# Attention values on column tiles of TensorE, with the result turned to tokens by the DMA crossbar

## The chip, the cores and the metric

The kernel runs on one core of one Trainium2 chip. The metric is the device time of one execution in microseconds, as the median over runs. The core has five engines that run their own instruction lists and meet at semaphores: TensorE (PE in the profile, with its weight loads as PEld), VectorE (DVE), ScalarE (ACT), GpSimd (POOL) and SyncE (SP), which here only issues DMAs.

## The reference

Two layers, each an attention block and a feed-forward block, over 2048 tokens of width 640. The attention has 32 heads of width 20 and cuts the tokens into 4 segments of 512. Inside a segment it is ordinary causal attention; what lies before a segment comes through a memory matrix per head:

```
x = x + A(layernorm(x)); x = x + B(layernorm(x))      # twice
A: q, k, v = x@wq, x@wk, x@wv        # 32 heads of 20
   for each segment s of 512 tokens:
     p     = softmax(q k^T / sqrt(20) + causal mask);  a_dot = p v
     a_mem = phi(q) M / (phi(q) z + 1e-6)              # phi(t) = t+1 for t>0, else exp(t)
     o     = g*a_mem + (1-g)*a_dot                     # g = sigmoid(beta) per head
     M += phi(k)^T v;  z += sum phi(k)
   return o @ wo
B: relu(x@w1) @ w2                   # 640 -> 1728 -> 640
```

All inputs and the output are bf16.

## The kernel before

Everything stays in SBUF between the stages; x is held as 16 tiles of 128 tokens (`x_sb`). The work goes by segment: normalise (`lnorm`, transposing the normed tokens to `xnT` by DMA), project to keys and queries with the features on partitions (`proj_kq`, line 712) and to values with the tokens on partitions (`proj_v`, line 746), score and apply, project the output (`out_proj`, line 1102), normalise again, and the feed-forward block (`ffn`, lines 1150 and 1170).

Heads are kept four to a group: keys and queries of head group g lie at partitions 0, 32, 64 and 96, 20 rows each. `scores` (line 978) takes two groups, a pair, in five rounds; a round is four or eight matmuls on four row tiles of the array, 512 columns in each tile, into PSUM banks 0 to 3. The scores come out with the keys on partitions. ScalarE takes the exponential (lines 994 and 998) into `PT`, of which there are two, one for each group of the pair, and GpSimd sets the part above the diagonal to zero (line 967). `PT` of one group holds four heads, and for each block j of 128 keys the queries from 128j on.

`apply` (line 1027) multiplies by the values. For a block i of 128 queries and a block j of 128 keys with j <= i, the 128x128 block of `PT` is the stationary operand, and the 20 values of the head with one more column (`v_aug`, whose last column gives the softmax sum, scaled so that the gate is in it) stream past: 40 matmuls with 21 columns for one group, into one PSUM bank (`OD`), with the tokens on partitions. VectorE takes the reciprocal of the sums (line 1042), multiplies (line 1050, or 1045 in a layer's first segment), and adds the product to the part that came from the memory (line 1055), in `o_sb`. When all eight groups of a segment are in, `o_turn` (line 1092) transposes `o_sb` to `oT` by DMA for `out_proj`.

The order of the instructions on each engine is fixed before the kernel runs, by a planner in the file (`Sched`, `paced`, `each`). Each stage is a stream of operations with a due time in units of a segment; the planner holds estimates of the duration of every operation, keeps a clock per engine, and always takes the operation that can start first, the one due first where several can start. A change of the array's tiling mode is booked at 100 ns (`MODE_NS`). Operations that would be in the way of a score round are put behind it (`RESERVE`). Scores and applies are due long before everything else; normalising and the projections of segment k are due 1.0 to 0.2 segments before it, the feed-forward block 1.4 to 2.4 segments after. Besides, a segment's normalising waits until the scores of the segment two before have begun, and until one of two `xnT` places is free. Buffers are slots that a stage takes and drops: two for `PT`, one for `OD`, three banks (`MISC`) for all other PSUM results, three sets of keys, queries and values, three normed tiles (`NXN`). SP issues all transposes, the relay of the last three key groups through DRAM (`relay`, lines 774 and 787) and the output, in the planned order, and waits at each for what it needs.

Of the kernel before, what the change touches and what calls it, by code (L numbers as in the profile page):

```python
# [11 lines left out]
H = 32  # L12
# [146 lines left out]


class Sched:
# [66 lines left out]
    def _best(self, op, resv=None):  # L228
# [140 lines left out]
def bass_interleave_layers__memory_aug_infini_attn__dense_activation_relu__prompt_kernel(  # L369
    nc, A_x, A_wq, A_wk, A_wv, A_wo, A_beta, B_x, B_w1, B_w2, out,  # L370
):
    with contextlib.ExitStack() as es:
# [6 lines left out]
        NXT, NXN, NET = 3, 3, 2  # L379
# [10 lines left out]
        NKQ, NVA = 2 * 5 * L, NJ * H * E1  # L390
        kq_0 = wb[:, W1N:W1N + NKQ].rearrange("p (n c f) -> p n c f", n=2, c=5)
        va_0 = wb[:, W1N + NKQ:W1N + NKQ + NVA].rearrange("p (j h e) -> p j h e", j=NJ, h=H)
# [18 lines left out]
        va_12 = sb("va_12", [128, 2, NJ, H, E1])  # L411
        v_aug = [va_0, va_12[:, 0], va_12[:, 1]]
# [7 lines left out]
        otmp = sb("otmp", [128, 2, NJ, 4, DH])  # L420
        rden = sb("rden", [128, 2, NJ, 4, 1], dt.float32)
# [22 lines left out]
        OTMP = [Slot(otmp[:, k], "otmp") for k in range(2)]  # L444
# [7 lines left out]
        ktk_sem = [sem_("kt%d" % k) for k in range(3)]  # L452
        ot_sem = [sem_("ot%d" % k) for k in range(2)]
# [98 lines left out]
        def consts():  # L552
# [4 lines left out]
            S.set("ident", v=[t1])  # L557
            th = yield pool(150, lambda e: e.memset(nhalf[:], -0.5))
# [8 lines left out]
            for b in range(3):  # L567
                t = yield pool(400, lambda e, b=b: e.tensor_copy(
                    v_aug[b][:, :, :, DH:E1], gt[:, 1, :][:, None, :, None].to_broadcast([128, NJ, H, 1])), [ta])
                VA[b][0].drop(t)  # L570
# [373 lines left out]
        def scores(m):  # L944
# [27 lines left out]
            for u, parts in enumerate(rounds):  # L972
# [10 lines left out]
                items = sorted({x for x, _, _ in parts})  # L983
                w = []
# [27 lines left out]
        def apply(n):  # L1012
# [10 lines left out]
            tk = od = None  # L1023
            for i in range(NJ):
                def make(bank, i=i, x=n % 2):
                    od = bank[:, 0:336].rearrange("p (i hh e) -> p i hh e", i=NJ, hh=4)
                    return [(lambda e, i=i, hh=hh, j=j: e.matmul(  # L1027
                        od[:, i, hh, :], PT[:, x, hh, PT_OFF[j] + 128 * (i - j):PT_OFF[j] + 128 * (i - j) + 128],
                        v_aug[b][:, j, 8 * hh + g, :], start=(j == 0), stop=(j == i)),
                        i == NJ - 1 and hh == 3 and j == i) for hh in range(4) for j in range(i + 1)]  # L1030
                if od is None:
# [225 lines left out]
```

## Time and profile before

| | |
|---|---|
| Median of 3 runs | 639.55 us (639.46 to 642.18) |
| Profiled execution | 639.16 us, span 637.4 us, mean granted clock 0.973 |
| PE | 593.1 us busy, 93% of the span |
| ACT | 424.7 us, 67% |
| DVE | 392.7 us, 62% |
| POOL | 197.8 us, 31% |
| DMA queue of SP | 32.5 MB, 29.6% of the 16 engines' span |

"Busy" is the time in which the engine had an instruction under way. Matmuls are pipelined: each is shown with its whole latency, while the next begins long before it ends, so 93% is not 93% of what PE could stream. In a row of a group stand the engine, the operation, what it writes and reads with the shapes, the number of instructions, the total busy time and the mean of one in ns, and behind the second bar the idle time of the engine just before them with what ended it. "xnT<-xn_tok" is a write of `xnT` that reads `xn_tok`.

### The profile page before, as it was taken

To read this page: it belongs to the slowest core of one execution; us is meant where nothing else is said; L and a number is where in the kernel's file an instruction comes from. 1 tells how busy PE (TensorE), PEld (TensorE's weight loads), DVE (VectorE), ACT (ScalarE), POOL (GpSimd) and SP (SyncE) were. 2 spreads that over 40 slices of the span, in tenths; PEclk is the share of its full clock that TensorE was granted. 3 is DMA by queue.
4 is the path that set the end of the run, shared out by engine and by line. 5 is a ranking of instruction groups with operands and counts; after the bars stand their busy time and mean duration, and the time that the engine had idled before them with its cause. 6 is when DMAs were issued, how large, how long until landed. Compare 5 with 4: busy or idle time off the path is not lost.

```text
span 637.4 us, 15205 instructions
## 1 busy us (share of the span) xinstructions
PE 593.1 (93%) x6498; PEld 337.8 (53%) x6498; DVE 392.7 (62%) x995; ACT 424.7 (67%) x512; POOL 197.8 (31%) x318
## 2 busy tenths in 40 slices
PE   6868998699999999999999999999999999999798
PEld 3344554354565566545664556645565556646445
DVE  7457768884588469646765567867586465735302
ACT  4576977787867766678677857878578756780040
POOL 3244344533334334333433313333233322330000
PEclk9878997899999999999999999999999999999799
DMA  6398749620322152222712426023530126004201
GB/s 196 92 173 155 116 102 174 126 51 16 72 48 59 15 91 33 48 38 37 121 24 43 75 32 98 11 43 75 87 84 11 22 25 113 33 1 63 63 0 42
DMA packets 101940, 43.17 MB, mean 68 GB/s; under 512 B 88416, under 2 KB 100576, under 8 KB 101872
## 3 DMA queue, kind: packets, MB, share of 16 engines
q1 hardware_dynamic: 98240, 32.52, 29.6%
q0 software_dynamic: 1520, 7.21, 4.0%
q10 hardware_dynamic: 2112, 2.47, 1.1%
q8 instruction: 51, 0.84, 0.5%
q14 instruction: 17, 0.14, 0.1%
HBM read 14.26 MB, written 6.55 MB: 33 GB/s over the span
## 4 chain that ended last, share of the span: by engine, by line
PE 73%; DVE 11%; ACT 7%; DMA 5%; POOL 2%; issue 1%; SPq 0%; DVEq 0%
PE ps L1150 18%; PE ps L1170 16%; PE ps L712 11%; PE ps L1027 9%; PE ps L978 7%; PE ps L1102 6%; PE ps L746 5%; ACT PT L998 4%; DMA oT<-o_sb 2%; DMA xnT<-xn_tok 2%; DVE x_sb L1065 1%; DVE xn_tok L627 1%; POOL rstd L623 1%; DVE stats L615 1%; POOL PT L967 1%
## 5 line engine op out<-in xcount | busy, mean ns | idle before, releaser
L998 ACT ACTIVATE PT<-ps 128x1024 bf16<-128x1024 f32 x256 | 248.1, 1022 | 90.2 <-PE ps L978 89.6
L967 POOL TENSOR_SCALAR_AFFINE_SELECT PT<-PT 128x512 bf16<-128x512 bf16 x256 | 162.0, 650 | 340.8 <-ACT PT L998 302.0
L1150 PE MATMUL ps<-xnT,wb 128*128 128x512 bf16 x560 | 150.6, 385 | 6.0 <-DMA xnT<-xn_tok 4.2
L1170 PE MATMUL ps<-wb,hT 128*128 128x320 bf16 x896 | 138.2, 299 | 3.7 <-DVE o_sb L914 2.5
L1170 PEld LDWEIGHTS ps<-wb,hT 128*128 128x128 bf16 x896 | 82.6, 98 | 43.0 <-issue 7.8
L1065 DVE TENSOR_TENSOR x_sb<-x_sb,ps 128x320 bf16<-128x320 bf16 x128 | 60.7, 479 | 62.1 <-PE ps L1170 50.5
L1150 PEld LDWEIGHTS ps<-xnT,wb 128*128 128x128 bf16 x560 | 51.7, 99 | 68.2 <-issue 16.5
L1134 ACT ACTIVATE hT<-ps 128x512 bf16<-128x512 f32 x69 | 41.3, 598 | 62.2 <-PE ps L1150 61.5
L746 PE MATMUL ps<-wv_r,xnT 128*128 128x320 bf16 x320 | 73.1, 306 | 3.5 <-ACT xnT L643 2.3
L1027 PEld LDWEIGHTS ps<-va,PT 128*128 128x128 bf16 x2240 | 64.1, 96 | 13.2 <-POOL PT L967 5.3
L994 ACT ACTIVATE PT<-ps 128x1024 bf16<-128x1024 f32 x64 | 62.0, 1022 | 12.1 <-PE ps L978 12.1
L1027 PE MATMUL ps<-va,PT 128*128 128x21 bf16 x2240 | 65.2, 173 | 2.6 <-POOL PT L967 2.5
L712 PE MATMUL ps<-xnT,wk_p 128*128 128x512 bf16 x200 | 63.8, 396 | 0.9 <-ACT xnT L643 0.8
L1042 DVE RECIPROCAL rden<-ps 128x16 f32<-128x16 f32 x64 | 16.2, 254 | 77.7 <-PE ps L1027 77.7
L712 PE MATMUL ps<-xnT,wq_p 128*128 128x512 bf16 x200 | 60.8, 387 | 0.9 <-DVE kq L699 0.9
L1102 PE MATMUL ps<-wo_r,oT 128*128 128x320 bf16 x320 | 54.1, 308 | 6.3 <-DMA oT<-o_sb 2.9
L699 DVE CAST kq<-ps 128x512 bf16<-128x512 f32 x54 | 36.8, 685 | 20.2 <-PE ps L712 20.0
L627 DVE TENSOR_SCALAR xn_tok<-x_sb,mv,rstd 128x640 bf16<-128x640 bf16 x64 | 33.0, 526 | 25.8 <-POOL rstd L623 17.3
L746 PEld LDWEIGHTS ps<-wv_r,xnT 128*128 128x128 bf16 x320 | 30.4, 99 | 28.2 <-issue 4.9
L1102 PEld LDWEIGHTS ps<-wo_r,oT 128*128 128x128 bf16 x320 | 29.3, 99 | 25.3 <-DMA oT<-o_sb 4.7
L1133 DVE TENSOR_SCALAR hT<-ps 128x512 bf16<-128x512 f32 x43 | 29.7, 690 | 19.7 <-PE ps L1150 19.4
L978 PE MATMUL ps<-kq 20*128 20x512 bf16 (+3 forms) x560 | 36.1, 308 | 2.8 <-ACT PT L998 2.6
(79 smaller groups left out, 548.2 us busy)
## 6 DMA issues: line engine op xcount, KB each, us to landing
kqL<-kq_scr SPq DMA_DIRECT2D x32, 120.0 KB
kq_scr<-kq SPq DMA_DIRECT2D x28, 120.0 KB
out_dram<-x_sb SPq DMA_DIRECT2D x16, 160.0 KB, 1.8
wb<-in_B_w_dram POOLq DMA_DIRECT2D x5, 432.0 KB, 6.7
x_sb<-in_A_x_dram POOLq DMA_DIRECT2D x3, 640.0 KB, 5.1
wb<-in_B_w_dram POOLq DMA_DIRECT2D x2, 640.0 KB, 6.6
xnT<-xn_tok SPq DMA_TRANSPOSE x60, 2.7
wv_r<-in_A_wv_dram ACTq DMA_DIRECT2D x1, 800.0 KB, 6.0
```

The lines of the kernel that those rows point to most:

```text
L712: fn = lambda e, bank, k=k, w_p=w_p, c=c: e.matmul(bank, w_p[:, k, c * 128:(c + 1) * 128], xnT[:, k_, :, k, :], start=(k == 0), stop=(k == ...
L746: fn = lambda e, bank, k=k, i=i, hf=hf: e.matmul(bank[:, 0:320], xnT[:, k_, i, k, :], wv_r[:, k, hf * 320:(hf + 1) * 320], start=(k == 0), ...
L967: tm = yield pool(590.0, lambda e: e.affine_select(out=reg, in_=reg, pattern=[[0, 4], [1, 128]], compare_op=ALU.is_ge, fill=0.0, base=0, c ...
L978: fns.append((lambda e, x=x, j=j, hh=hh, N=N, o=o: e.matmul(ps[:, hh, o:o + N], kq(b, gg[x], 0)[32 * hh:32 * hh + DH, 128 * j:128 * j + 12 ...
L994: fn = lambda e, k=k, bp=bs.ap: e.activation(PT[:, :, 2 * k:2 * k + 2, 1024:1280], bp.rearrange("p h (x t) -> p x h t", x=2), ACT.Exp, sca ...
L998: fn = lambda e, k=k, bp=bs.ap, x=items[0], c0=c0: e.activation(PT[:, x, 2 * k:2 * k + 2, c0:c0 + 512], bp, ACT.Exp, scale=SCALE)
L1027: return [(lambda e, i=i, hh=hh, j=j: e.matmul(od[:, i, hh, :], PT[:, x, hh, PT_OFF[j] + 128 * (i - j):PT_OFF[j] + 128 * (i - j) + 128], v ...
L1065: ta = yield dve(320, 1, lambda e: e.tensor_tensor(xa, xa, bk.ap[:, 0:320], ALU.add), [tk], early=HOT)
L1102: fn = lambda e, bank, k=k, hf=hf, o=ot.ap: e.matmul(bank[:, 0:320], o[:, k, :], wo_r[:, k, hf * 320:(hf + 1) * 320], start=(k == 0), stop ...
L1134: lambda e: e.activation(hTv[:, dc, :], bk.ap, ACT.Relu), [tk] + hs.old)
L1150: fn = lambda e, bank, k=k, dc=dc: e.matmul(bank, w1_r[:, k, dc * 128:(dc + 1) * 128], xnT[:, k_, :, k, :], start=(k == 0), stop=(k == FC ...
L1170: fn = lambda e, bank, dc=dc, i=i, hf=hf: e.matmul(bank[:, 0:320], hTv[:, dc, i * 128:(i + 1) * 128], w2_r[:, dc, hf * 320:(hf + 1) * 320] ...
```

## The change

The operands of the apply change places. For head hh of the group and key block j, the values are now the stationary operand: 32 columns from the head's first value on, that is its 20 values, its sum column and 11 columns that belong to the next head and come out unused. They sit in column tile hh of the array (128 rows, 32 columns), and write to PSUM partitions 32hh to 32hh+31. The streaming operand is `PT` of the block, with all queries from 128j on: 512, 384, 256 and 128 columns for j = 0 to 3. So an apply is 16 matmuls, four in each column tile, marked as mode "col". The result has head and feature on partitions and the tokens along the free dimension. So that the 32 columns of the last head don't run out of the buffer, each value buffer is 16 elements longer, zeroed by GpSimd at the start.

The result must be turned to tokens. `turn` evacuates the bank to bf16 (`oraw`, on VectorE or ScalarE, whichever the planner finds sooner), and when both groups of a pair are there, one DMA transpose of 128x1024 (`XK`) brings them to `otok` with the tokens on partitions. Then come one reciprocal for both groups, and in a layer's first segment two products into `o_sb`, else one product in place and two sums.

In the planner, a column operation that finds the array in the full mode is ranked 3 us later (`PATIENCE`), so that it tends to come behind a score round. A pair's score rounds take each of the two `PT` halves when they first write it, where before both were taken ahead of the first round. Normalising, projections and relay are due 1.5 segments earlier. One of the three normed tiles is gone.

```diff
+PATIENCE = 3000.0
@@ Sched._best
             if e == "pe" and op.mode != self.mode:
                 start = max(self.free[e] + MODE_NS, r)
+                if op.mode == "col" and self.mode == "full":
+                    rank = max(rank, r + PATIENCE)
@@ buffers
-        NXT, NXN, NET = 3, 3, 2
+        NXT, NXN, NET = 3, 2, 2
-        NKQ, NVA = 2 * 5 * L, NJ * H * E1
+        NKQ, NVA = 2 * 5 * L, NJ * H * E1 + 16
-        otmp = sb("otmp", [128, 2, NJ, 4, DH])
-        rden = sb("rden", [128, 2, NJ, 4, 1], dt.float32)
+        oraw = sb("oraw", [128, 2, 2, L])
+        otok = sb("otok", [128, 2, 2 * NJ, 4, 32])
+        rden = sb("rden", [128, 2, 2 * NJ, 4, 1], dt.float32)
@@ scores
-            for x in range(2):
-                yield Op([("act", 0.0, 0.0, lambda: [])], [], hold=[PTS[x][0]])
-            pold = [PTS[x][0].old for x in range(2)]
+            pold = [None, None]
...
                 items = sorted({x for x, _, _ in parts})
+                for x in items:
+                    if pold[x] is None:
+                        yield Op([("act", 0.0, 0.0, lambda: [])], [], hold=[PTS[x][0]])
+                        pold[x] = PTS[x][0].old
@@ apply
-            for i in range(NJ):
...
+            x = n % 2
+            def make(bank):
+                return [(lambda e, hh=hh, j=j: e.matmul(
+                    bank[32 * hh:32 * hh + 32, 128 * j:L],
+                    v_flat[b][:, (j * H + 8 * hh + g) * E1:(j * H + 8 * hh + g) * E1 + 32],
+                    PT[:, x, hh, PT_OFF[j]:PT_OFF[j] + L - 128 * j], start=(j == 0), stop=(j == NJ - 1)),
+                    j == NJ - 1 and hh == 3) for j in range(NJ) for hh in range(4)]
+            tk, od = yield pe(25.0 + 1280 / 2.4, make, mk + vt, [OD], mode="col")
...
+            S.spawn(turn(n, a, s, g, od, tk), "turn")
+        def turn(n, a, s, g, od, tk):
+            x = n % 2
+            if x == 0:
+                te, rw = yield evac(512, 1, lambda e, d: e.tensor_copy(d[:, 0, :], od.ap),
+                                    lambda e, d: e.activation(d[:, 0, :], od.ap, ACT.Copy), [tk], [ORAW])
+                od.drop(te)
+                S.set("raw", n, v=[rw, te])
+                return
+            rw, t0 = yield Need("raw", n - 1)
+            te = yield evac(512, 1, lambda e: e.tensor_copy(rw.ap[:, 1, :], od.ap),
+                            lambda e: e.activation(rw.ap[:, 1, :], od.ap, ACT.Copy), [tk] + rw.old)
+            od.drop(te)
+            tx, ok = yield XK(rw, [t0, te])
+            rw.drop(tx)
+            ov = otok[:, ok.ap]
+            tr, rd = yield dve(240, 1, lambda e, d: e.reciprocal(d, ov[:, :, :, DH:E1]), [tx], [RDEN])
+            ob = yield Need("ob", a, s)
+            num = ov[:, :, :, 0:DH]
...
+            if s == 0:
...
+            else:
+                tm = yield dve(640, 1, lambda e: e.tensor_tensor(
+                    num, num, rd.ap.to_broadcast([128, 2 * NJ, 4, DH]), ALU.mult), [tr])
+                om = yield Need("omem", a, s, g // 4)
...
+        class XK(Op):
+            def __init__(self, rw, waits):
+                super().__init__([("sp", 200.0 + 27.0 * 64, 0.0, self.make)], waits, [OTOK], 1)
+                self.dma = [None, 900.0, 1700.0]
...
+                return [(lambda e: e.dma_start_transpose(
+                    otok[:, k].rearrange("p c r e -> p c (r e)"), rw.ap.rearrange("p x t -> p (x t)")), True)]
@@ due times
-        each(ln1, "ln1", -1.0, -0.8, 24)
-        each(proj_kq, "kq", -0.8, -0.3, 60)
-        each(relay, "relay", -0.4, -0.3, 8)
-        each(proj_v, "v", -0.8, -0.2, 48)
+        each(ln1, "ln1", -2.5, -2.3, 24)
+        each(proj_kq, "kq", -2.3, -1.8, 60)
+        each(relay, "relay", -1.9, -1.8, 8)
+        each(proj_v, "v", -2.3, -1.7, 48)
```

More of the change, by code (lines that the diff above doesn't have):

```diff
@@ L443, in bass_interleave_layers__memory_aug_infini_attn__dense_activation_relu__prompt_kernel @@
         OSB = [[Slot(o_sb[:, k], "osb")] for k in range(2)]
-        OTMP = [Slot(otmp[:, k], "otmp") for k in range(2)]
+        ORAW = [Slot(oraw[:, k], "oraw") for k in range(2)]
+        OTOK = [Slot(k, "otok") for k in range(2)]
         RDEN = [Slot(rden[:, k], "rden") for k in range(2)]
@@ L557, in consts @@
             S.set("ident", v=[t1])
+            tv0 = []
+            for b in range(3):
+                tk = yield pool(100, lambda e, b=b: e.memset(v_flat[b][:, NJ * H * E1:NVA], 0.0))
+                tv0.append(tk)
             th = yield pool(150, lambda e: e.memset(nhalf[:], -0.5))
@@ L1022, in apply @@
             va, vt = vt[0], vt[1:]
-            tk = od = None
-            for i in range(NJ):
[L1025 to L1031, printed above, removed]
-                    _, od = yield pe(26.0 * 4, make, mk + vt, [OD])
-                else:
-                    tk = yield pe(26.0 * 4 * (i + 1), lambda make=make, bank=od.ap: make(bank))
+            x = n % 2
[6 more added lines that the diff above has]
+            tk, od = yield pe(25.0 + 1280 / 2.4, make, mk + vt, [OD], mode="col")
             pt.drop(tk)
```

51 lines of the change are left out of this document (27 added, 24 removed).

## The prediction

> **What bounds the kernel now.** I read the page's head first (span, engines, the chain of work that ended last), then busy time in stretches of the span.
>
> ```profile
> span 637.4 us, 15205 instructions
> PE 593.1 (93%) x6498; PEld 337.8 (53%) x6498; DVE 392.7 (62%) x995; ACT 424.7 (67%) x512; POOL 197.8 (31%) x318
> PE 73%; DVE 11%; ACT 7%; DMA 5%; POOL 2%; issue 1%; SPq 0%; DVEq 0%
> ...
> 20.00:140.00 120.00, 101.82 (x1136) 53.40 (x1135) 86.47 (x215) 89.82 (x106) 47.91 (x74) 0.89 0.65 129
> 140.00:580.00 440.00, 429.10 (x5002) 248.63 (x4999) 276.86 (x698) 317.45 (x374) 141.90 (x224) 1.00 0.29 50
> 580.00:637.40 57.40, 49.70 (x303) 29.77 (x300) 15.56 (x39) 8.36 (x14) 1.27 (x2) 0.93 0.19 42
> ```
>
> The columns of the last three rows are PE, PEld, DVE, ACT and POOL busy, then granted clock, DMA share and GB/s. From 140 to 580 us PE is busy 429 of 440 us at full clock: there the matmul stream itself sets the time, and a microsecond taken out of it should come off the end. The start (18 us idle, clock 0.89) and the tail (8 us idle, clock 0.93) have other limits. Inside the middle stretch the scores do stop at times, shown by the exponentials of L998, but PE is given other work:
>
> ```profile
> 340.00:360.00 20.00, 10.61 (x12) 1.00 0.27 54
> 360.00:380.00 20.00, 3.88 (x4) 1.00 0.35 51
> ```
>
> So the attention can be late while PE is full.
>
> **The apply on PE.** The next rows are pieces of the chain (start, length, what), then the groups.
>
> ```profile
> 69.76 0.33 PE ps L978 x4
> 71.06 0.99 PE ps L1027 x40
> 142.75 2.16 PE ps L1150 x10
> ...
> L1027 PE MATMUL ps<-va,PT 128*128 128x21 bf16 x2240 | 65.2, 173 | 2.6 <-POOL PT L967 2.5
> L1027 PE MATMUL ps<-wb,PT 128*128 128x21 bf16 x320 | 9.5, 175 | 4.4 <-POOL PT L967 4.4
> ```
>
> Removed: 2560 matmuls, 64 applies of 40, each with a load of a full 128x128 block and only 21 columns streamed. One apply is 0.99 us, 25 ns a pair. Added: 64 sets of 16 matmuls, four column tiles side by side, each streaming 512, 384, 256 and 128 columns: 1280 columns per tile. Ten matmuls of 512 take 2.16 us, so 0.216 us per 512 columns, and 1280 columns take 0.54 us if the four tiles stream at once. No row of before shows column tiles. The nearest are the four row tiles of a score round:
>
> ```profile
> 261.89 0.12 PEld L978 LDWEIGHTS ps<-kq 20*128 20x128 bf16 x8 [0.26 <-ACT PT L998]
> 261.89 0.40 PE L978 MATMUL ps<-kq 20*128 20x384 bf16 x8
> 267.09 0.39 PE L978 MATMUL ps<-kqL 20*128 20x512 bf16 x4
> ```
>
> Four matmuls of 512 last 0.39 us together, and eight (384 and 128 in each tile) last 0.40 us: the tiles overlap, and the second load of a tile is hidden. In the chain such a round takes 0.33 us for 0.216 us of columns, so a change of mode costs about 0.11 us. An apply beside a score round adds one change (rows to columns in place of rows to full): 0.54 + 0.11 = 0.65 us. One that the planner puts alone, after the 3 us of patience, adds two: 0.76 us. Saving: 0.34 x 64 = 22 us, or 0.23 x 64 = 15 us if all were alone. The bounds from below: four tiles one after another would make it 2.16 us plus 0.11, a loss of 82 us; the row tiles speak against that. I take 22, since the score round no longer waits for both halves of PT and so one is nearly always near.
>
> [...]
>
> **The way out of PSUM.** Groups: total busy, mean ns.
>
> ```profile
> L1042 DVE RECIPROCAL rden<-ps 128x16 f32<-128x16 f32 x64 | 16.2, 254 | 77.7 <-PE ps L1027 77.7
> L1050 DVE TENSOR_TENSOR otmp<-ps,rden 128x320 bf16<-128x320 f32 x48 | 23.4, 487 | 1.2
> L1055 DVE TENSOR_TENSOR o_sb<-o_sb,otmp 128x320 bf16<-128x320 bf16 x48 | 18.2, 385 | 0.7
> L1045 DVE TENSOR_TENSOR o_sb<-ps,rden 128x320 bf16<-128x320 f32 x16 | 7.8, 488 | 0.4
> L1133 DVE TENSOR_SCALAR hT<-ps 128x512 bf16<-128x512 f32 x43 | 29.7, 690 | 19.7 <-PE ps L1150 19.4
> L1134 ACT ACTIVATE hT<-ps 128x512 bf16<-128x512 f32 x69 | 41.3, 598 | 62.2 <-PE ps L1150 61.5
> ```
>
> Removed from DVE: 16.2 + 23.4 + 18.2 + 7.8 = 65.6 us. Added per pair: one reciprocal (32 elements, between 0.25 and 0.5 us: I take 0.33), in six pairs of eight one product of 640 (between once and twice 0.487: 0.82) and two sums (0.385 each), in the others two products of 0.48: 32 x 0.33 + 24 x 1.59 + 8 x 0.96 = 56 us, a gain of 9. Added too are 64 evacuations of 512 columns, 0.69 us on DVE or 0.60 on ACT; shared evenly that is +22 on DVE and +19 on ACT. DVE ends near 405 us, ACT near 444. I cost both at nothing: in the middle stretch PE's stream hides them, with ACT busy 317 and DVE 277 of 440 us. If the cover is gone, they cost up to the 19 us of ACT. The PSUM bank of the output is free after one evacuation instead of a reciprocal and a product (0.6 to 0.7 against 0.74), so the next apply waits no longer.
>
> The 32 crossbar transposes of 128x1024 stand between these rows, in SP's issue (640 columns, then 1536) and in landing:
>
> ```profile
> 593.47 1.21 SPq L666 DMA_TRANSPOSE xnT<-xn_tok  x1
> 93.92 1.77 SPq L820 DMA_TRANSPOSE ktok<-kqL  x1
> xnT<-xn_tok SPq DMA_TRANSPOSE x60, 2.7
> ktok<-kqL SPq DMA_TRANSPOSE x6, 3.9
> ...
> 112.23 9.74 SPq L654 DMA_TRANSPOSE xnT<-xn_tok  x2
> ```
>
> By the columns, 1.45 us of SP and 3.2 us to landing; SP gets 46 us more, spread over the span. Each makes SP wait for its evacuation with the next segment's transposes, the key relay and the output transposes behind it, and makes DVE's reciprocal wait for the landing with evacuations behind it. The planner books 1.93 + 0.9 + 1.7 = 4.5 us for it, more than the 3.2, so in the middle stretch neither queue should stand. Before 140 us it can: there the DMA share is 0.65 and two transposes held SP 9.74 us.
>
> **The start and the earlier projections.** In 100 to 125 us PE had little to do, and the third segment's projections began only at 124.6 us:
>
> ```profile
> 98.25 0.40 PE L978 MATMUL ps<-kq 20*128 20x256 bf16 x8
> 100.78 0.98 PE L1102 MATMUL ps<-wo_r,oT 128*128 128x320 bf16 x3 [2.14 <-DMA oT<-o_sb]
> 113.08 1.52 PE L1102 MATMUL ps<-wo_r,oT 128*128 128x320 bf16 x10 [1.57 <-DVE otmp L1050]
> 124.62 0.61 PE L712 MATMUL ps<-xnT,wk_p 128*128 128x512 bf16 x1
> 100.00:120.00 20.00, 13.65 (x168) 7.66 (x168) 16.25 (x48) 12.17 (x15) 7.87 (x12) 0.83 0.76 134
> 120.00:140.00 20.00, 17.90 (x198) 8.96 (x199) 17.85 (x43) 16.28 (x19) 9.62 (x14) 0.83 0.43 89
> ```
>
> These two windows lose 8.4 us idle and 0.17 x 40 = 7 us to the clock. Due 1.5 segments sooner, the norm of the third segment may go ahead of DVE's other work and its projections fill that hole: up to -13 us. Against it, the slower way out makes the first output projection about 4.5 us later and eight more transposes go through the crowded queue: up to +8. I take -4. Elsewhere the new dues only exchange feed-forward work for projections on a full PE: zero, with more feed-forward left for the tail. The two normed tiles instead of three cost a landing more per segment (about 1.2 us), hidden by PE's other work except at the end.
>
> **The tail.**
>
> ```profile
> 575.71 0.26 DVE L1042 RECIPROCAL rden<-ps 128x16 f32<-128x16 f32 x1 [3.05 <-PE ps L1027]
> 576.53 0.33 DVE L1055 TENSOR_TENSOR o_sb<-o_sb,otmp 128x320 bf16<-128x320 bf16 x1
> ...
> 589.29 7.23 PE L1170 MATMUL ps<-wb,hT 128*128 128x320 bf16 x52
> ...
> 600.69 17.81 PE L1150 MATMUL ps<-xnT,wb 128*128 128x512 bf16 x70 [4.17 <-DMA xnT<-xn_tok]
> ```
>
> From the last apply to the summed output: 1.15 us. After: evacuation 0.7, transpose 3.2, then 0.33 + 0.82 + 0.77: 5.8, so 4.6 later, and 1.2 for the normed tiles. If no more feed-forward is left than now, that is +5.8. If the attention ends further ahead, leftover feed-forward work covers it, and also removes the 4.17 us wait and the slow clock behind it (70 matmuls in 17.81 us against 15.1 at 0.216): -6.9. I lean to the second, since scores and projections now go first: -3.
>
> **Sum.** 637.4 - 22 - 4 - 3 = 608.4 of span; the profiled execution took 639.16, 1.8 us more than its span and 0.4 under the median of 639.55. With these 1.8: 610. The planner's order was made for other durations than the chip's, so I add 2 for queues that stand: **612 us**.
>
> **The rivals.**
> - A, column tiles share the reading of what streams: four tiles run as two at a time. It shows on the apply alone and decides from 0.99 us per apply: 1.08 + 0.11 = 1.19 us, +0.20 x 64 = +13 us, and the two others' -7 would hardly come, as the attention is later: 637.4 + 13 + 1.8 = 652. For it: no row of column tiles; against: the row tiles, which stream four at once, though from 20 rows each. Slower than before.
> - B, loads are exposed: each of the four steps waits for a load as long as the rows show one, 96 ns for L1027. 0.54 + 4 x 0.096 + 0.11 = 1.03 us, +3 us in all; with half of the -7: 639. [...] Against it: the eight-load round that took 0.40 us.
> - C, PE is freed but the attention doesn't come forward: the longer way out and the crossbar queue give back 8 at the start and 5.8 in the tail: 637.4 - 22 + 13.8 + 1.8 = 631.
> - D, the holes close: -22 - 13 - 6.9: 597.
>
> **Chances.** Forecast 0.50 (its own range 603 to 624), A 0.13 (a full serial run, 82 us, is in it with 0.03), B 0.11, C 0.14, D 0.12. About 0.5% (3.2 us) is what a measurement can tell from no change. Faster: 0.50 + 0.12 + 0.13 of C + 0.02 of B = 0.77; same: 0.07; slower: 0.16. The range goes from D's 597 to 641, past B, and leaves out A and a little below.
>
> **What would show it.** Apply pieces of 16 matmuls of about 0.55 us in the chain, next to a piece of L978; 0.11 us gaps at each side. PE busy near 570 us. Evacuations of `oraw` of 0.6 to 0.7 us on both engines, transposes of 3 to 3.5 us to landing. PE busy in 100 to 140 above 34 of 40 us. In the tail, `L1170` work of more than 112 matmuls after the last apply and no wait before the last `L1150` row. The forecast is wrong if an apply takes over 0.8 us, if PE idles over 20 us in 140 to 560, or if the last apply stays at 575 us.

## The result, and the profile after

The changed kernel takes 602.79 us (median of 4 runs, 601.62 to 606.37); in the same comparison the kernel before takes 639.5. The ratio is 0.943, with a 95% interval of 0.938 to 0.947, so 36.7 us or 5.7% less. The profiled execution took 602.58 us. The forecast was 612 us with a range of 597 to 641. The sign was right and the gain was 9 us larger than forecast; 602.79 lies just below the 603 to 624 that the forecast case itself was given.

First the head of the page after (span, engines, the chain that ended last), then busy time in stretches of the span, with the columns as before (PE, PEld, DVE, ACT, POOL, granted clock, DMA share, GB/s).

```profile
span 600.8 us, 12152 instructions
PE 565.5 (94%) x4962; PEld 293.6 (49%) x4962; DVE 414.9 (69%) x990; ACT 430.1 (72%) x525; POOL 205.9 (34%) x321
PE 74%; DVE 15%; ACT 5%; DMA 3%; POOL 1%; issue 1%; DVEq 0%
...
20.00:140.00 120.00, 100.70 (x881) 45.05 (x879) 86.89 (x198) 95.28 (x112) 55.61 (x82) 0.89 0.69 138
140.00:560.00 420.00, 414.49 (x3784) 219.93 (x3783) 308.27 (x736) 317.53 (x382) 143.53 (x217) 1.00 0.41 72
560.00:600.80 40.80, 37.34 (x233) 22.43 (x230) 5.85 (x12) 8.36 (x14) 0.00 (x0) 1.00 0.08 29
```

PE has 27.6 us less work (593.1 to 565.5) and stands still for 9.0 us less (44.3 to 35.3 us, span less busy time). The start is as it was: 19.3 us idle in 20 to 140, at the same mean clock of 0.89. The middle idles 5.5 us in 420. The last stretch runs at full clock, where before it had 0.93.

The middle as PE's timeline shows it (start, length, engine, line, operation, what the engine waited for):

```profile
303.08 0.40 PE L989 MATMUL ps<-kqL 20*128 20x384 bf16 x8
303.40 0.50 PEld L1041 LDWEIGHTS ps<-PT,va 128*32 128x32 bf16 x16 [0.21 <-issue]
303.41 0.73 PE L1041 MATMUL ps<-PT,va 128*32 128x512 bf16 x16
304.07 0.82 PE L725 MATMUL ps<-xnT,wk_p 128*128 128x512 bf16 x3
```

An apply stands directly behind a score round. From its start to the start of the next row it takes 0.66 us, and its sixteen loads are done within 0.50 us of that. The apply's row is shown with 0.73 us, past the start of the next one, so I read the starts. From start to start, the whole timeline gives: before, 30 applies stood between other matmuls of the full array and took 1.01 us each; after, 61 of the 64 stand right behind a score round, and 57 of these take 0.66. Behind the other four 1.4 to 4.1 us pass: two run at a granted clock of 0.50 (at 36.51 and 99.18 us) with a wait behind them, and two (at 43.35 and 109.59 us) have only the wait.

The groups that answer to the costs in the prediction, then the row of the DMA issues (median us from issue to landing) and one of SP's timeline:

```profile
L1057 DVE CAST oraw<-ps 128x512 bf16<-128x512 f32 x32 | 21.7, 678 | 9.5 <-PE ps L1041 9.3
L1063 DVE CAST oraw<-ps 128x512 bf16<-128x512 f32 x30 | 20.6, 687 | 16.5 <-PE ps L1041 16.4
L1064 ACT ACTIVATE oraw<-ps 128x512 bf16<-128x512 f32 x2 | 1.2, 597 | 0.4 <-PE ps L1041 0.3
L1069 DVE RECIPROCAL rden<-otok 128x32 f32<-128x32 bf16 x32 | 10.9, 342 | 6.6 <-DMA otok<-oraw 6.6
L1077 DVE TENSOR_TENSOR o_sb<-otok,rden 128x320 bf16<-128x320 bf16 x16 | 7.8, 527 | 0.1
L1082 DVE TENSOR_TENSOR otok<-otok,rden 128x640 bf16<-128x640 bf16 x24 | 21.0, 874 | 0.1
L1087 DVE TENSOR_TENSOR o_sb<-o_sb,otok 128x320 bf16<-128x320 bf16 x48 | 14.7, 360 | 0.2
...
otok<-oraw SPq DMA_TRANSPOSE x32, 3.3
...
60.80 1.31 SPq L1104 DMA_TRANSPOSE otok<-oraw  x1
```

The prices of the way out were near the estimates (reciprocal 0.34 against 0.33, product 0.87 against 0.82, sum 0.36 against 0.385, transpose 3.3 to landing against 3.2, 1.31 of SP against 1.45). But 62 of the 64 evacuations went to DVE; the planner didn't share them.

The tail, from the last apply to the end: the timeline's row of the apply, then the chain of waits.

```profile
510.45 0.73 PE L1041 MATMUL ps<-PT,va 128*32 128x512 bf16 x16
...
544.94 5.84 PE ps L1196 x27
551.45 15.39 PE ps L1216 x112
566.84 15.12 PE ps L1196 x70
582.64 15.40 PE ps L1216 x112
```

The last apply starts at 510.5 us, where before it was at 574.5. What follows is feed-forward work without a wait, and the last 70 matmuls of the first product take 15.12 us, not 17.81 behind a wait of 4.17.

The score rounds show what else changed. Before, 18 pairs of neighbouring rounds lay over 5 us apart, some 127 us together: most at the ends of pairs, and the three longest (15 us each) behind a segment's first pair. After, there are 3, some 46 us together, of which one is long (358.96 to 393.66): the second layer's third segment needs its own feed-forward result of the first layer, whose last matmuls run at 356.8, its projections begin at 388.38, and PE does feed-forward work meanwhile. The attention ends 64 us earlier in a kernel that is 37 us shorter; the experiments show what these pauses have to do with it.

### The profile page after: what moved, and what is told of

It reads as the page before. It is cut to its first block, busy times and chain, and to the rows that moved or that the text cites. A ratio compares the mean times of both kernels' runs of the same rounds, so it can differ in the third digit from the quotient of the medians.

```text
span 600.8 us, 12152 instructions
## 1 busy us (share of the span) xinstructions
PE 565.5 (94%) x4962; PEld 293.6 (49%) x4962; DVE 414.9 (69%) x990; ACT 430.1 (72%) x525; POOL 205.9 (34%) x321
## 3 DMA queue, kind: packets, MB, share of 16 engines
q1 hardware_dynamic: 132032, 40.92, 39.3%
## 4 chain that ended last, share of the span: by engine, by line
PE 74%; DVE 15%; ACT 5%; DMA 3%; POOL 1%; issue 1%; DVEq 0%
PE ps L1216 19%; PE ps L1196 16%; PE ps L725 13%; PE ps L1148 7%; PE ps L989 7%; PE ps L759 6%; PE ps L1041 5%; ACT PT L1013 3%; DMA oT<-o_sb 2%; DVE stats L627 1%; DVE stats L628 1%; DVE x_sb L1111 1%; DVE xn_tok L640 1%; DVE hT L1179 1%; ACT etmp L841 1%; POOL rstd L636 1%
## 5 line engine op out<-in xcount | busy, mean ns | idle before, releaser
L978 POOL TENSOR_SCALAR_AFFINE_SELECT PT<-PT 128x512 bf16<-128x512 bf16 x256 | 170.9, 685 | 273.4 <-ACT PT L1013 232.1
L1216 PE MATMUL ps<-wb,hT 128*128 128x320 bf16 x896 | 132.1, 299 | 3.0 <-ACT hT L1180 1.8
L1196 PE MATMUL ps<-xnT,wb 128*128 128x512 bf16 x560 | 132.8, 380 | 0.3 <-DVE hT L1179 0.3
L1196 PEld LDWEIGHTS ps<-xnT,wb 128*128 128x128 bf16 x560 | 51.6, 98 | 61.6 <-issue 5.8
L759 PE MATMUL ps<-wv_r,xnT 128*128 128x320 bf16 x320 | 64.7, 311 | 3.8 <-ACT xnT L656 1.5
L725 PE MATMUL ps<-xnT,wk_p 128*128 128x512 bf16 x200 | 56.3, 384 | 1.3 <-ACT xnT L656 0.8
L725 PE MATMUL ps<-xnT,wq_p 128*128 128x512 bf16 x200 | 55.9, 386 | 0.0
L712 DVE CAST kq<-ps 128x512 bf16<-128x512 f32 x43 | 29.2, 680 | 20.0 <-PE ps L725 19.8
L1041 PE MATMUL ps<-PT,va 128*32 128x128 bf16 (+3 forms) x896 | 41.3, 305 | 0.7 <-POOL PT L978 0.7
L1063 DVE CAST oraw<-ps 128x512 bf16<-128x512 f32 x30 | 20.6, 687 | 16.5 <-PE ps L1041 16.4
L627 DVE BATCH_NORM_STATS2 stats<-x_sb 128x6 f32<-128x320 bf16 x64 | 30.5, 476 | 1.5 <-DMA x_sb<-in_A_x_dram 0.8
L628 DVE BATCH_NORM_STATS2 stats<-x_sb 128x6 f32<-128x320 bf16 x64 | 30.4, 474 | 0.0
```

The costliest lines, as they stand in the source:

```text
L725: fn = lambda e, bank, k=k, w_p=w_p, c=c: e.matmul(bank, w_p[:, k, c * 128:(c + 1) * 128], xnT[:, k_, :, k, :], start=(k == 0), stop=(k == ...
L759: fn = lambda e, bank, k=k, i=i, hf=hf: e.matmul(bank[:, 0:320], xnT[:, k_, i, k, :], wv_r[:, k, hf * 320:(hf + 1) * 320], start=(k == 0), ...
L978: tm = yield pool(590.0, lambda e: e.affine_select(out=reg, in_=reg, pattern=[[0, 4], [1, 128]], compare_op=ALU.is_ge, fill=0.0, base=0, c ...
L1041: return [(lambda e, hh=hh, j=j: e.matmul(bank[32 * hh:32 * hh + 32, 128 * j:L], v_flat[b][:, (j * H + 8 * hh + g) * E1:(j * H + 8 * hh + ...
L1196: fn = lambda e, bank, k=k, dc=dc: e.matmul(bank, w1_r[:, k, dc * 128:(dc + 1) * 128], xnT[:, k_, :, k, :], start=(k == 0), stop=(k == FC ...
L1216: fn = lambda e, bank, dc=dc, i=i, hf=hf: e.matmul(bank[:, 0:320], hTv[:, dc, i * 128:(i + 1) * 128], w2_r[:, dc, hf * 320:(hf + 1) * 320] ...
```

## The experiments

Two readings of the gain had to be told apart. **Stream:** PE's matmul stream sets the time, the applies are 0.35 us cheaper, and 64 of them make 22 us; the rest is small change. **Order:** how early the scores come (each half of `PT` taken by itself) and whether PE has other work by then (the due times) decide whether a freed microsecond is seen at all.

### Old due times in the changed kernel

```diff
-        each(ln1, "ln1", -2.5, -2.3, 24)
-        each(proj_kq, "kq", -2.3, -1.8, 60)
-        each(relay, "relay", -1.9, -1.8, 8)
-        each(proj_v, "v", -2.3, -1.7, 48)
+        each(ln1, "ln1", -1.0, -0.8, 24)
+        each(proj_kq, "kq", -0.8, -0.3, 60)
+        each(relay, "relay", -0.4, -0.3, 8)
+        each(proj_v, "v", -0.8, -0.2, 48)
```

> The changed kernel, with normalising, projections and relay due as before. Theory S (PE's stream sets the time, so each part counts for what it does to the stream): the apply stays 0.66 us, at most the tail's wait and slow clock come back (6.9 us): 603 to 610. Theory O (the freed PE time counts only where the attention comes forward, and the due times bring it forward): scores stand at the segments' ends again, the last apply is past 545 us instead of 511, PE waits in the tail: 622 to 636.

Measured: 640.97 us, ratio to before 1.003 (1.000 to 1.007). The whole gain is gone. The windows and the tail row of this kernel, then rows from the end of a long pause between score rounds:

```profile
20.00:140.00 120.00, 95.38 (x867) 41.55 (x865) 92.85 (x217) 95.32 (x109) 53.96 (x81) 0.84 0.72 140
140.00:560.00 420.00, 406.27 (x3631) 208.96 (x3628) 298.91 (x689) 305.90 (x364) 140.32 (x212) 1.00 0.38 67
560.00:638.20 78.20, 62.16 (x403) 35.82 (x401) 22.91 (x52) 15.56 (x24) 4.77 (x7) 0.91 0.17 39
...
601.25 18.01 PE L1196 MATMUL ps<-xnT,wb 128*128 128x512 bf16 x70 [10.88 <-DMA xnT<-xn_tok]
...
232.47 0.71 PE L759 MATMUL ps<-wv_r,xnT 128*128 128x320 bf16 x4
...
236.75 0.73 PE L1041 MATMUL ps<-PT,va 128*32 128x512 bf16 x16
237.41 0.40 PE L989 MATMUL ps<-kq 20*128 20x512 bf16 x4
```

An apply still takes 0.66 us, so the stream is as cheap as in the changed kernel, but PE idles 61.6 us (638.2 less 576.6 busy) instead of 35.3: 24.6 in the start, 13.7 in the middle, 16.0 at the end, where a wait of 10.9 us stands before the last product. The saving of the applies is real and shows as idle time. Stream alone is refuted. The last three rows show what the due times move. Five long pauses between score rounds, of 9 to 24 us, each begin behind a segment's first pair. In the one shown the fourth segment's last values are projected at 232.5 to 233 us, its first apply follows, and only then, with `PT` free, the next score round, 23.8 us after the one before. With the new due times the same values are ready at 155 us, and the scores don't stop there.

### New due times in the kernel before

The same four lines the other way round, in the kernel before.

> The kernel before, with only the new due times. Theory S: no PE work is taken away, so 639 within 3 us, the tail's 6.9 at most. Theory O: little as well, since a pair's first round still waits for both halves of PT: 632 to 639. If the due times alone were worth what the sum lacked, 628 or less.

Measured: 638.48 us, ratio 0.999 (0.995 to 1.002). Nothing: 22 pauses of over 5 us between score rounds are still there. Due times alone bring nothing either.

### No patience

```diff
-PATIENCE = 3000.0
+PATIENCE = 0.0
```

> The changed kernel with a patience of 0. Applies stand alone more often, each with one change of mode more (0.11 us): if all did, 7 us. Theory S: 603 to 610, with a share of applies between full-mode matmuls that times 0.11 us gives the difference. Theory O: up to 7 more if the attention ends later: 606 to 615.

Measured: 615.31 us, ratio 0.962 (0.958 to 0.967), 12.5 us above the changed kernel. Now 56 of 64 applies stand between matmuls of the full array. An apply still takes 0.66 us to the next row, and the change of mode that the score round shared with it is paid elsewhere: 56 changes of 0.11 us are 6 us. PE is busy for 571.3 us of a span of 612.9, so 5.8 us longer than in the changed kernel, and idle for 6.3 us more; this other half of the 12.5 comes with a later attention, whose last apply starts at 534 us, 24 us later.

### Both PT halves taken ahead of a pair, as before

```diff
-            pold = [None, None]
+            for x in range(2):
+                yield Op([("act", 0.0, 0.0, lambda: [])], [], hold=[PTS[x][0]])
+            pold = [PTS[x][0].old for x in range(2)]
...
-                for x in items:
-                    if pold[x] is None:
-                        yield Op([("act", 0.0, 0.0, lambda: [])], [], hold=[PTS[x][0]])
-                        pold[x] = PTS[x][0].old
```

> The changed kernel, but a pair's first score round again takes both halves of PT. Theory S: applies are no longer beside a score round, 0.11 us each: 603 to 610. Theory O: the second apply of a pair waits 3 us of patience for a score round that itself waits for that apply, so each of 32 pairs is later by 2 to 3 us and the attention ends 60 to 80 us later: 640 to 680, slower than before the change.

Measured: 689.24 us, ratio 1.077 (1.070 to 1.084): slower than the kernel before. One pair's end in PE's timeline:

```profile
314.18 0.40 PE L991 MATMUL ps<-kqL 20*128 20x384 bf16 x8
314.50 0.73 PE L1039 MATMUL ps<-PT,va 128*32 128x512 bf16 x16
315.16 4.49 PE L1194 MATMUL ps<-xnT,wb 128*128 128x512 bf16 x20
320.34 0.85 PE L1214 MATMUL ps<-wb,hT 128*128 128x320 bf16 x5 [0.69 <-ACT hT L1178]
321.13 0.73 PE L1039 MATMUL ps<-PT,va 128*32 128x512 bf16 x16
321.79 0.40 PE L991 MATMUL ps<-kq 20*128 20x512 bf16 x4
```

The next pair's first round (321.79) must wait for the second group's apply (321.13), and that apply waits for the exponentials and the mask of the round at 314.18 (the mask ends at 317.84), and then for its patience. The scores pause 7.6 us, after nearly every pair (29 pauses over 5 us), and the exponentials wait for them. The groups of the exponentials (busy, mean ns, idle before them), of this kernel and of the changed one:

```profile
L1011 ACT ACTIVATE PT<-ps 128x1024 bf16<-128x1024 f32 x256 | 248.1, 1021 | 119.4 <-PE ps L991 118.8
```

```profile
L1013 ACT ACTIVATE PT<-ps 128x1024 bf16<-128x1024 f32 x256 | 248.2, 1024 | 46.9 <-PE ps L989 46.3
```

The work is the same and ScalarE waits 72 us more for scores. The kernel before has the same hold with some 5 us a pair. So the split of the halves, which the prediction passed over in a clause, is a part that the column apply with its patience can't do without.

### The split and the due times, with the old apply

The two edits to the order made in the kernel before: the halves of `PT` taken one by one, and the new due times.

> The kernel before (apply of 40 matmuls), with the two planner parts that do not touch the apply: the PT halves taken one by one, and the new due times. In the run with the old due times the shorter apply alone gave nothing, and the new due times alone gave nothing on the kernel before; so two limits lie close together, PE's stream and the pace of the attention. Theory T (two limits): this one lifts the pace only and is left with the stream, so it is slower than the changed kernel by the applies, 0.35 x 64 = 22 us: 620 to 630, gaps of over 5 us between score rounds mostly gone. Rival (the order alone carries the gain): 600 to 608. Rival (the stream carries it): 635 or more.

Measured: 625.55 us, ratio 0.978 (0.974 to 0.982). It is 22.8 us above the changed kernel, and the applies' difference is 64 x 0.35 = 22.4. So with this order in both kernels the stream reading gives the difference, though the way out and the patience are in it too, and nothing here shows that they add up to zero by themselves.

### The split alone

```diff
-            for x in range(2):
-                yield Op([("act", 0.0, 0.0, lambda: [])], [], hold=[PTS[x][0]])
-            pold = [PTS[x][0].old for x in range(2)]
+            pold = [None, None]
...
                 items = sorted({x for x, _, _ in parts})
+                for x in items:
+                    if pold[x] is None:
+                        yield Op([("act", 0.0, 0.0, lambda: [])], [], hold=[PTS[x][0]])
+                        pold[x] = PTS[x][0].old
```

> The kernel before with only one edit: a pair's score rounds take each PT half when they first write it. Apply and due times stay as before. Theory T (the attention's pace and the work that fills PE must both change): the pauses of 5 us at the pair ends go, but at the ends of the segments PE runs out of other work, so pauses of 10 to 25 us between score rounds stay there and the time is 633 to 641. Rival S (the split alone frees the attention, and the due times add nothing): 623 to 628, as with the due times (625.6).

Measured: 625.58 us, ratio 0.981 (0.976 to 0.986): as with the new due times. My expectation was wrong, and rival S right. Long pauses are there as expected (five of 17 to 22 us, though behind a segment's first pair and not at its end), but they cost this kernel little, because PE has feed-forward work in them and still enough of it for the tail. The first and the last stretch of this kernel:

```profile
20.00:140.00 120.00, 106.59 (x1304) 56.51 (x1303) 89.90 (x227) 100.48 (x118) 54.69 (x83) 0.90 0.68 130
...
560.00:619.40 59.40, 55.17 (x352) 34.07 (x350) 16.72 (x40) 10.92 (x19) 1.27 (x2) 1.00 0.17 44
```

So with the old apply the split brings 14 us and the due times nothing; with the column apply the due times bring 38 (641.0 to 602.8).

### Two normed tiles, and patience under the old due times

The column apply with the old due times (641.0) is 15 us slower than the old apply with the same order (625.6), though each of its applies is 0.35 us shorter. Two runs asked what eats this. The first puts `NXN = 2` into the split kernel, the second puts `PATIENCE = 0` into the changed kernel with the old due times.

> The kernel before with the PT halves taken one by one (625.6 us) and two normed tiles in place of three. The changed kernel with the old due times takes 641.0, 15 us more than the split alone, though its applies are 22 us cheaper. Theory N (the two normed tiles, a landing more in each segment, cost the changed kernel much of this): 633 to 641. Rival (they cost nothing, as forecast except at the end): 624 to 628.

> The changed kernel with the old due times and PATIENCE = 0. Theory P (the 3 us of patience makes the applies late, and with the old due times nothing makes up for it): under 634. Rival W (the loss lies in the longer way out of PSUM, with its crossbar transposes and DVE work, and in work that comes too late to fill PE): the 7 us of additional mode changes come on top, 641 to 655.

Measured: 623.15 us (ratio 0.976, 0.973 to 0.978) and 641.97 us (1.005, 1.002 to 1.007). Two normed tiles cost the old apply nothing. Taking the patience away brings no time back beside the old due times either, though it isn't cleared altogether: the first apply behind the fourth segment's last values comes 3.9 us after them with patience and 1.0 us without, and the 51 additional changes of mode, 5.6 us of PE's time, may have used up such a gain. Otherwise what is left is the way out itself (the evacuation, the transpose and the DVE work on both sides of it) or the traffic that it adds; no run here takes it away alone, so the cause stays open. Where the time goes can be read: the long pauses begin at 206, 274, 346, 418 and 493 us in the split kernel and at 214, 289, 362, 428 and 504 us in this one, and the last apply at 556 and 571. So 15 us are already lost by 290 us, and the lag is 9 to 16 us from there on. The fourth segment's key and query projections begin at 145.6 us in the one and at 193.2 in the other. In 20 to 140 us PE is busy for 106.6 us at clock 0.90 in the split kernel, and for 95.4 at 0.84 in this one.

### More stream

In the changed kernel, the four matmuls with 512 columns run twice in each apply; the second set restarts the sums.

```diff
-                    PT[:, x, hh, PT_OFF[j]:PT_OFF[j] + L - 128 * j], start=(j == 0), stop=(j == NJ - 1)),
-                    j == NJ - 1 and hh == 3) for j in range(NJ) for hh in range(4)]
+                    PT[:, x, hh, PT_OFF[j]:PT_OFF[j] + L - 128 * j], start=(j == 0), stop=(w in (0, NJ))),
+                    w == NJ and hh == 3) for w, j in enumerate((0, 0, 1, 2, 3)) for hh in range(4)]
```

> The changed kernel with the first four matmuls of each apply run twice (the first time thrown away), in the same order of all instructions: 0.216 us more of PE's stream per apply, 13.8 us in all. If PE's stream sets the changed kernel's end: 614 to 618. If the pace of the attention sets it and PE has room: 603 to 608. An apply should take 0.87 us.

Measured: 614.42 us, ratio 0.961 (0.957 to 0.965): 11.6 us more for 64 x 0.216 = 13.8 us of stream. In the timeline the applies take 64.1 us in all instead of 49.8. In the changed kernel five sixths of the added stream came out as time.

### Dearer evacuations

Each evacuation of `oraw` in four instructions of 128 columns, on the same engine one behind the other, booked by the planner as the one instruction before.

```diff
-                te, rw = yield evac(512, 1, lambda e, d: e.tensor_copy(d[:, 0, :], od.ap),
-                                    lambda e, d: e.activation(d[:, 0, :], od.ap, ACT.Copy), [tk], [ORAW])
+                te, rw = yield quarters(od, None, 0, [tk], [ORAW])
...
-            te = yield evac(512, 1, lambda e: e.tensor_copy(rw.ap[:, 1, :], od.ap),
-                            lambda e: e.activation(rw.ap[:, 1, :], od.ap, ACT.Copy), [tk] + rw.old)
+            te = yield quarters(od, rw.ap, 1, [tk] + rw.old, [])
```

> The changed kernel with each evacuation of the output bank in four instructions of 128 columns, in the same order. By the row of 512 columns (0.68 us, 0.53 of it for the columns) a quarter takes about 0.28, so each evacuation 0.43 us more, 27 us more on DVE in all. If PE's stream hides the way out: 601 to 606. If DVE is a second limit: up to 630.

Measured: 608.78 us, ratio 0.952 (0.949 to 0.956), 6.0 us above the changed kernel. The group and the two windows of this kernel:

```profile
L1061 DVE CAST oraw<-ps 128x128 bf16<-128x128 f32 x248 | 54.2, 280 | 25.5 <-PE ps L1041 24.9
...
20.00:140.00 120.00, 96.50 (x854) 43.03 (x852) 84.85 (x231) 91.24 (x107) 54.64 (x80) 0.87 0.70 137
140.00:560.00 420.00, 413.22 (x3759) 216.44 (x3758) 317.15 (x883) 322.23 (x393) 144.83 (x219) 1.00 0.41 70
```

Four quarters take 1.12 us where one evacuation took 0.68, 0.44 more on each path. The two means, 280 ns for 128 columns and 678 for 512, leave an estimated 1.04 ns a column, 0.53 us for 512, as the expectation had it. PE loses 4.2 us of work in the start (100.70 to 96.50) and 1.3 in the middle. So the cover that I relied on holds in the middle, and is thin in the start, where PE isn't full.

### The matmuls of an apply in another order

```diff
-                    j == NJ - 1 and hh == 3) for j in range(NJ) for hh in range(4)]
+                    j == NJ - 1 and hh == 3) for hh in range(4) for j in range(NJ)]
```

> The changed kernel with the 16 matmuls of an apply head by head (four key blocks of one column tile, then the next tile) in place of key block by key block over the four tiles. Same matmuls, same loads. If tiles only overlap when their matmuls stand next to each other in the list: about 4736 columns one after another, 2.0 us an apply in place of 0.66, +86 to +95 us: 685 to 700. If each tile runs on its own: 0.66, 603.

Measured: 604.48 us, ratio 0.946 (0.942 to 0.950): as the changed kernel. All four matmuls of one column tile now stand ahead of the first of the next, and the apply takes the same time (0.69 us here from start to start):

```profile
302.19 0.53 PEld L1041 LDWEIGHTS ps<-PT,va 128*32 128x32 bf16 x16 [0.21 <-issue]
...
302.19 0.76 PE L1041 MATMUL ps<-PT,va 128*32 128x512 bf16 x16
302.88 0.82 PE L725 MATMUL ps<-xnT,wk_p 128*128 128x512 bf16 x3
```

For tiles that overlap only where their matmuls stand next to each other in the list, the expectation's estimate was 2.0 us an apply; 0.69 were measured, so here the order in the list didn't decide what ran side by side.

### The second feed-forward weight later

In the changed kernel the loads of the second feed-forward weight wait for the first segment's second normalisation, so that they leave the crowded stretch from 95 to 125 us (DMA share 0.85 in the changed kernel).

```diff
+            r0 = yield Need("xm", 0, 0, 3)
-            w = w + [t for s in hold for t in s.old]
+            w = w + [t for s in hold for t in s.old] + [r0[1]]
```

> The changed kernel, with the loads of the second feed-forward weight (2.2 MB) held back until the first segment's second normalisation has reached xnT, so that they leave the stretch of 95 to 125 us, where the DMA share is near 0.9 and PE has a hole. Theory G (the hole is there because the fourth segment's projections wait for the scores of the segment two before and for its buffers): PE busy in 100 to 140 us stays at 30.6 of 40 within 1.5 us, and the time is 600 to 607. Theory D (the crowded DMA engines delay the transposes, and these the hole): PE busy in 100 to 140 us rises above 33, and the time is 594 to 600. Where the loads then come too late for the first feed-forward product, the time is above 607 and PE busy falls.

Measured: 618.56 us, ratio 0.968 (0.964 to 0.972). The stretch from 100 to 140 us, first of the kernel before, then after, then of this one:

```profile
100.00:140.00 40.00, 31.54 (x366) 16.62 (x367) 34.10 (x90) 28.45 (x33) 17.48 (x26) 0.83 0.60 111
```

```profile
100.00:140.00 40.00, 30.61 (x277) 13.90 (x269) 33.94 (x82) 30.16 (x35) 20.53 (x28) 0.86 0.75 143
```

```profile
100.00:140.00 40.00, 27.73 (x256) 11.82 (x255) 33.99 (x88) 30.63 (x35) 18.33 (x25) 0.67 0.60 98
```

The DMA share fell from 0.75 to 0.60, and PE had less work, not more. A less crowded DMA doesn't fill the hole, which speaks against theory D; since the late weights disturb this run too, it doesn't settle the matter. PE busy also fell by more than G allowed; the time is the third case of the expectation, weights that come too late.

### What the runs say together

| Apply | PT halves | Due times | us |
|---|---|---|---|
| old | both | old | 639.5 |
| old | both | new | 638.5 |
| old | one by one | old | 625.6 |
| old | one by one | new | 625.6 |
| column | both | new | 689.2 |
| column | one by one | old | 641.0 |
| column | one by one | new | 602.8 |

"Column" stands for the new apply with all that came with it: the way out, the patience and the two normed tiles. Column with both halves and the old due times was not run. Read along one path, the split is worth 14 us, the due times behind it 0, and the column apply 23; along another path the column apply loses 15 and the due times bring 38. The parts don't add up, because PE's saved time counts only where the scores come early enough and other work is at hand.

## Why the prediction was right, and where it was not

**What bounds the kernel.** "From 140 to 580 us ... the matmul stream itself sets the time, and a microsecond taken out of it should come off the end." Half right. It holds for the most part in the changed kernel (the run with more stream: 11.6 of 13.8 us). It fails as a law: with the old due times 22 us of stream went and the end stayed. A PE that is 97% busy was a sign that work was at hand under that order, not that it would be under another.

**The apply, -22.** Right: 0.66 us against a forecast of 0.65, and 0.35 x 64 = 22.4 us. The four column tiles stream at once, so rival A (652 us) falls. Rival B, exposed loads (1.03 us an apply), falls too: sixteen loads, shown with 97 ns each in the mean, lie within 0.50 us of an apply's 0.66. No load is seen in the time: an estimated 0.54 of columns (from 0.216 per 512) and 0.11 for the change of mode (from the 0.33 us of a score round) make 0.65 of the 0.66.

**The way out, at nothing.** Right in sum, wrong in where. I shared the evacuations evenly and forecast DVE at 405 and ACT at 444; 62 of 64 went to DVE, and the engines ended at 414.9 and 430.1. The cover holds in the middle; the quarters, 0.44 us more on each evacuation, cost 6 us in all, most of it in the start. One row was misread: the 9.74 us in which two transposes seemed to hold SP were mostly a wait. The first of them took 1.27 us, and the tokens of the second were written only at 120.35 us.

**The start, -4.** Wrong, this step failed: PE's busy time in 100 to 140 us was to rise above 34 of 40 and went from 31.5 to 30.6; idle time in 20 to 140 rose by 1.1. The projections that I wanted in the hole began at 124.62 before and at 123.90 after. The reading of the code was at fault: they are those of the fourth segment, and its tokens reach SBUF late. Their load stands behind that of the first feed-forward weight, and no due time was changed for it. The rows of the load and of the first statistics of these tokens, before and then after:

```profile
83.70 0.79 POOL L497 DMA_DIRECT2D x_sb<-in_A_x_dram  x1
90.11 0.48 DVE L614 BATCH_NORM_STATS2 stats<-x_sb 128x6 f32<-128x320 bf16 x1
```

```profile
84.23 0.79 POOL L506 DMA_DIRECT2D x_sb<-in_A_x_dram  x1
94.83 0.48 DVE L627 BATCH_NORM_STATS2 stats<-x_sb 128x6 f32<-128x320 bf16 x1
```

The load lands 5.5 us after its issue before and 4.7 us after, so at 89 us in both, and the statistics can't begin sooner: an earlier place in the order could have brought them forward by 1 us before and 6 us after. The projections begin 1.3 and 1.7 us behind the landing of the last transpose of these tokens (123.3 and 122.2 us); what fills the 34 and 29 us from the first statistics to the projections is open. Theory G named the scores of the segment two before as the gate. In the traces these begin at 93.1 us before, 3 us behind the statistics, and at 83.0 after, 12 us ahead of them, so after the change at least they didn't hold the statistics. The set of buffers that G named too isn't tested, and no run here loads these tokens earlier.

**The due times elsewhere, "zero".** Wrong, and the largest miss in the reasoning: beside the new apply and the split they are worth 38 us. Beside the old apply they are worth nothing, which is what my sentence described. I costed the parts one by one against the kernel before, and didn't ask whether a segment's values are ready when its first apply comes.

**The split of PT**, which I used only as a reason why a score round is near, was worth 14 us by itself. I had seen its sign: the exponentials' stops at 340 to 380 us and "the attention can be late while PE is full". I didn't ask what else would happen when the attention is no longer late.

**The tail, -3.** The mechanism that I leaned to was right and its full size came: the attention ended further ahead, leftover feed-forward work covered its end, and the 4.2 us wait and 2.7 us of slow clock went, -6.9. The sign named for it was badly chosen: more than 112 matmuls of the second product (line 1170) stood behind the last apply before the change already, 224, and after it 336 (line 1216). That no wait stands before the last 70 of the first product did tell.

**The 2 us for standing queues** were not seen. The middle idles 5 us less than before (10.5 to 5.5 us in 140 to 560).

In sum: -22.4 for the applies, -6.9 for the tail, +1.1 for the start and -5 for the middle make -33.2 of the -36.6 in span. By lines, from start to start, the applies and the scores together give -26.0, the second feed-forward product (with the wait that stood behind it) -8.0, and all other lines -2.6. Rival C (the attention doesn't come forward, 631 us) describes the kernel with the old due times, which came out 10 us worse still. Rival D's 597 us needed the hole closed. The forecast of 612 was near partly by luck: a start that gave nothing stood against a tail and a middle that gave more, and the 22 us of the applies came off the end only because the due times, put at zero, and the split were in the same change.

## What to carry to other kernels

When an engine is 97% busy under a fixed order, ask not only what a cheaper operation saves but what the engine will do with the time: look for the other stream that runs at its own pace (here the scores, held by a buffer's release) and for the supply of work behind it. Price edits that belong together as one, since alone they may be worth zero or less. And before moving a due time to fill a hole, find what the work in question really waits for: a load of its input, a gate or a buffer isn't moved by a due time.

## What the runs showed of the hardware

- Four column tiles of 128 rows and 32 columns streamed side by side, and the order in the instruction list made little difference: head by head an apply took 0.69 us and the kernel 604.48, against 0.66 and 602.79 us. Tile after tile, the 5120 columns would be an estimated 2.16 us, from 0.216 per 512. In the run with more stream, 512 columns more in each of the four tiles made an apply 0.22 us longer, as 512 columns take 0.216 in the full array.
- The column tiles of an apply all use the same 128 rows, and their loads were hidden all the same: sixteen loads with a mean of 97 ns, an estimated 1.55 us end to end, were done within 0.50 us, and an apply took 0.66.
- The mean duration of one matmul in these records isn't what the operation cost where tiles ran side by side. One of 512 columns is shown with 0.39 us in a column tile and with 0.38 in the full array, and the row of the group says:

```profile
L1041 PE MATMUL ps<-PT,va 128*32 128x128 bf16 (+3 forms) x896 | 41.3, 305 | 0.7 <-POOL PT L978 0.7
```

  896 of 305 ns would be 273 us, where the group is busy for 41.3.
- The 32 crossbar transposes of 128x1024 from SBUF to SBUF landed 3.0 to 6.2 us after their issue, 3.3 in the median, and held SP for 1.24 us in the median (1.31 in the row shown, 2.66 at most). SP's hardware DMA queue moved 40.9 MB where before it moved 32.5, and the time of its packets rose from 29.6% to 39.3% of 16 engines' span.
